# Float32 attention heads by pairs, on the whole TensorE array, in a fused attention and FFN kernel

## The chip, the cores and the metric

The kernel runs on one core of one Trainium2 chip. The metric is device time in microseconds (us) for one execution of the whole program, from loading the inputs to storing the output. The engines of the core are named as in the profile: PE (TensorE matmul), PEld (TensorE's weight loads), DVE (VectorE), ACT (ScalarE), POOL (GpSimd) and SP (SyncE, which here issues nearly all DMA loads and stores).

## The reference, cut to what matters

An attention with a local window and 32 global tokens runs over 8 batches and 8 heads of size 64, with 512 local positions; an FFN with a squared ReLU runs over its 4608 rows.

```python
k_all = concatenate([k_g, k_l]); v_all = concatenate([v_g, v_l])
out_g = softmax(scale * q_g @ k_all.T) @ v_all            # 32 global rows see everything
s_ll  = where(abs(pos_i - pos_j) <= 32, scale * q_l @ k_l.T, -1e9)
s_lg  = scale * q_l @ k_g.T
out_l = softmax(concatenate([s_lg, s_ll])) @ v_all        # local rows see a window and the globals
x = concatenate([out_g, out_l]) -> (4608, 512)            # heads side by side
h = x @ w_in                                              # 512 -> 2048
out = (s * relu(h) ** 2 + b) @ w_out                      # 2048 -> 512
```

All inputs and the output are float32.

## The kernel before, in words

**Steps and slots.** The attention is cut into 128 slots: slot `j` is batch `j // 16`, half `(j // 8) % 2` of the 512 local positions, and head `j % 8`. Each slot has 256 query rows in two blocks of 128, a window of keys of 416 columns in all (two blocks of 192 or 224, with the 32 global keys among them), and four pieces of values of 128 rows. The FFN is cut into 136 steps `m`, eight for each of 17 tiles of 256 rows: `ffn_in` (12 products for each of two groups of 128 hidden features) and `ffn_out`, and step `m` is written `LAG` = 12 slots after slot `m`. One loop over `j` writes all of this out; a scheduler then orders the instructions of each engine with a simulated time line and places the semaphores, so the order on an engine isn't quite the order of the loop.

**Two kinds of heads.** Most products split each float32 operand into a rounded part and a remainder and multiply these in the fast float32r format (`split`, `scores`, `p_split`, `pv_products`, `pv_sum`). The first `NF` = 16 slots (batch 0) don't: they multiply in plain float32, which needs no splitting on ACT, POOL and DVE, while each product is two passes on TensorE, counted as two instructions in the profile. These are the float32 heads, and the change touches only them. They run while the weights of the FFN are being prepared: `weight_piece` takes 32 pieces, two or three a slot over the first 14 slots (`PIECES`), from 64-bit floats to two float32r parts, with four operations on DVE (lines 143, 148, 152, 156), four on ACT or POOL and one more on POOL or DVE. Two pieces are loaded by ACT's queue, the others by SP's.

**One float32 head.** `load32` (line 252) loads the keys of a pair of heads into one tile of 128 partitions (the even head in partitions 0 to 63, the odd one in 64 to 127), and for each head its queries; the array `qd` holds the same queries in both halves of the partitions. `v_load32` (line 268) loads a head's values, 128 x 256. `scores32` (line 274) makes two products of the head's own 64 partitions of queries and keys (line 283) into the scores `ps_s`, and one product (line 289) of its 32 global queries and its own keys into `ps_g`; ACT copies the latter into the global scores `sg` (line 291). Ahead of it, while `j` < 12, four products of a constant tile keep TensorE busy (`keep_busy`, line 91). `softmax` (line 206) masks and scales on DVE (line 215), exponentiates on ACT (line 221), sums on DVE and normalises on POOL (line 228). `transposes32` turns the probabilities by four transposes (line 312), and ACT copies them to `pt` (line 320). `pv32` (line 323) multiplies values by probabilities in four products (line 329) of 64 output partitions, `p_o[0:64]`, and copies these to the head's 64 partitions of `x` (DVE for slots 0 to 7, line 337; ACT for 8 to 15, line 335).

**Buffers.** Score, global-score, transpose and output banks (tags `s`, `g`, `t`, `o`) have one buffer each; probabilities, their transposes and the values (`sm`, `pt`, `rv`) have two. The keys alternate between two tags, the queries as well. SP's queue issues in order, so a load that waits for its buffer holds those behind it.

**Around it.** `x_split` (before FFN tile 0, at slot 12) needs the outputs of slots 0 to 7; the global softmax and products of batch 0 follow slots 13 and 18. The functions that the diff touches:

Of the kernel before, what the change touches and what calls it, by code (L numbers as in the profile page):

```python
# [10 lines left out]
F32 = mybir.dt.float32  # L11
# [31 lines left out]
NF = 16  # L43
# [9 lines left out]
X_ACT = lambda j: j >= 8  # L53
# [11 lines left out]


@with_exitstack
def window_attention_then_ffn(ctx: ExitStack, tc: tile.TileContext, qd, qg, kw, vw, vg, w_in, w_out, sv, bv, out):
    nc = tc.nc
    scale = 1.0 / math.sqrt(D)  # L70

# [1 line left out]
    sb = ctx.enter_context(tc.tile_pool(name="sb", bufs=2))  # L73
    ps = ctx.enter_context(tc.tile_pool(name="ps", bufs=1, space=bass.MemoryType.PSUM))
# [22 lines left out]
    for first, parts in ((True, ((32, 192, 0),)), (False, ((0, 160, 0), (192, 224, 32)))):  # L97
# [108 lines left out]
    def softmax(j, p_s):  # L206
        b, hf, h = slot(j)
        sm = sb.tile([P, NC], F32, tag="sm", name=f"sm{j}")
        nm = sb.tile([P, 2], F32, tag="nm", name=f"nm{j}")
        ss = sb.tile([P, 2], F32, tag="ss", name=f"ss{j}")  # L210
        cols = [COLS[hf, blk] for blk in range(2)]
        for blk in range(2):
            c = cols[blk]
            mask = masks[hf == 0 and blk == 0][:, 0:c.stop - c.start]
            nc.vector.tensor_tensor_reduce(  # L215
                out=sm[:, c], in0=p_s[:, c], in1=mask,
                op0=ALU.add, op1=ALU.min, scale=-scale, scalar=BIG, accum_out=nm[:, blk:blk + 1],
            )
        for blk in range(2):
            p = sm[:, cols[blk]]  # L220
            nc.scalar.activation(  # L221
                out=p, in_=p, func=AF.Exp, bias=nm[:, blk:blk + 1], scale=-1.0, accum_out=ss[:, blk:blk + 1],
            )
        nc.vector.tensor_scalar_add(ss, ss, 1e-9)
        nc.vector.reciprocal(ss, ss)
        for blk in range(2):
            p = sm[:, cols[blk]]
            (nc.gpsimd if NORM_POOL(j) else nc.vector).tensor_scalar(  # L228
                out=p, in0=p, scalar1=ss[:, blk:blk + 1], scalar2=1.0, op0=ALU.mult, op1=ALU.mult,
            )  # L230
        st_["p", j] = sm


    def own(k, hf):
        n, c = (192, P) if hf == 0 else (240, 144)
        return k[:, 0:2 * n].rearrange("p (k c) -> p k c", k=2)[:, :, 0:c]

    def sg_rows(j):
        b, hf, h = slot(j)
        if hf == 0 and h % 4 == 0:  # L240
            st_["sg", b, h // 4] = sb.tile([P, SGW], F32, tag=f"sg{h // 4}", name=f"sg{j}", bufs=1)
        r0 = 32 * (h % 4)
        return st_["sg", b, h // 4][r0:r0 + 32]

    def x_tile(j):
        b, hf, h = slot(j)
        t = 2 * b + hf
        if h == 0:
            xcur[t] = sb.tile([P, 4, HALF], F32, tag="x", name=f"x{t}", bufs=1)
        return xcur[t]  # L250

    def load32(j):
        b, hf, h = slot(j)
        if h % 2 == 0:
            if j % 4 == 0:
                rk = sb.tile([P, 480], F32, tag="rk", name=f"rk{j}", bufs=1)
            else:
                rk = sb.tile([P, 10 * D], F32, tag="rvg", name=f"rk{j}", bufs=1)[:, 0:480]
            nc.sync.dma_start(rk[:, 0:NC], kw[b, hf, h // 2])
            st_["rk", j] = st_["rk", j + 1] = rk  # L260
        if j % 2 == 0:
            rq = sb.tile([P, HALF], F32, tag="rq", name=f"rq{j}", bufs=1)
        else:
            rq = sb.tile([P, 288], F32, tag="tg", name=f"rq{j}", bufs=1)[:, 0:HALF]
        nc.sync.dma_start(rq, qd[b, hf, h])
        st_["rq", j] = rq

    def v_load32(j):
        b, hf, h = slot(j)
        rv = sb.tile([P, 4 * D], F32, tag="rv", name=f"rv{j}")  # L270
        nc.sync.dma_start(rv, vw[b, hf, h])
        st_["rv", j] = rv

    def scores32(j):
        b, hf, h = slot(j)
        if WARM_HEAD and j < LAG:
            keep_busy(WARM_HEAD, f"warm{j + 1}")
        p = slice(64 * (h % 2), 64 * (h % 2) + 64)
        rk, rq = st_.pop(("rk", j)), st_.pop(("rq", j))
        p_s = ps.tile([P, 512], F32, tag="s", name=f"ps_s{j}")  # L280
        for blk in range(2):
            cols = COLS[hf, blk]
            nc.tensor.matmul(  # L283
                p_s[:, cols], lhsT=rq[p, blk * P:(blk + 1) * P], rhs=rk[p, cols], start=True, stop=True,
            )
        p_g = ps.tile([P, 512], F32, tag="g", name=f"ps_g{j}")
        qg = st_["rqg", b][p, h * SG:(h + 1) * SG]
        ng = 256 + 32 * hf
        nc.tensor.matmul(p_g[0:32, 0:ng], lhsT=qg, rhs=own(rk, hf)[p], start=True, stop=True)
        softmax(j, p_s)  # L290
        nc.scalar.copy(out=sg_rows(j)[:, hf * 256:hf * 256 + ng], in_=p_g[0:32, 0:ng])

    def chunks(j):
        b, hf, h = slot(j)
        o = 0
        for blk in range(2):
            for c in range(2):
                c0, q0, n = CHUNKS[hf, blk][c]
                yield blk, c, c0, q0, n, slice(o, o + n)
                o += n  # L300
# [22 lines left out]
    def pv32(j):  # L323
        b, hf, h = slot(j)
        pt, rv = st_.pop(("pt", j)), st_.pop(("rv", j))
        p_o = ps.tile([P, 2, 2, P], F32, tag="o", name=f"ps_o{j}")
        for blk, c, c0, q0, n, o in sorted(chunks(j), key=lambda x: (x[0], -x[1])):
            v = (2 * blk + c) * D
            nc.tensor.matmul(  # L329
                p_o[0:64, 0, blk, q0:q0 + n], lhsT=rv[:, v:v + D], rhs=pt[:, o], start=(c == 1), stop=(c == 0),  # L330
            )
        q0 = 64 * (h % 2)
        x_out = x_tile(j)[q0:q0 + 64, h // 2, :].rearrange("p (k q) -> p k q", k=2)
        if X_ACT(j):
            nc.scalar.copy(out=x_out, in_=p_o[0:64, 0])
        else:
            nc.vector.tensor_copy(out=x_out, in_=p_o[0:64, 0])
# [12 lines left out]
    def qg_split(b):  # L350
# [216 lines left out]
    for b in range(B):  # L567
        for g in range(2):
# [4 lines left out]
            for i in range(2):  # L573
                h = 4 * g + 2 * i
# [3 lines left out]
    def pick(f32_one, split_one):  # L578
# [18 lines left out]
    ld(1)
    for j in range(NM + LAG + 2):
# [6 lines left out]
        if j < NS:  # L605
            b1 = j // 16 + 1
            if j == 14 and NF > 16:
                qg_load32(1)
            elif j % 16 == 14 and b1 < B:
                qg_load(b1)  # L610
            sc(j)
            if j == NF - 1 and NF % 16:
                if NF > 16:
                    qg_load(j // 16)
                qg_split(j // 16)
            if j % 16 == 15 and NF <= j + 1 < NS:
                qg_split(b1)
# [93 lines left out]
```

## Time and profile before

| | |
|---|---|
| median of 3 runs | 1093.29 us (1093.09 to 1093.58) |
| profiled execution | 1092.8 us, span 1091.0 us |
| PE busy | 1052.7 us (96%) |
| PEld busy | 929.0 us (85%) |
| DVE busy | 858.8 us (79%) |
| ACT busy | 724.3 us (66%) |
| POOL busy | 418.3 us (38%) |
| mean granted TensorE clock | 0.974 |
| moved by DMA | 86.80 MB |

The span runs from the first to the last instruction. The granted clock is the share of full speed that TensorE was allowed; a busy TensorE at half clock does half the work. Rows for a group of instructions name the line, the engine, the operation, output and inputs with their shapes, how often, busy us and mean ns, and then the idle time of the engine just before them with what ended it. For a product, `64*128` says that 64 rows and 128 columns of the array are used.

### The profile page before, as it was taken

To read this page: it belongs to the slowest core of one execution; us is meant where nothing else is said; L and a number is where in the kernel's file an instruction comes from. 1 tells how busy PE (TensorE), PEld (TensorE's weight loads), DVE (VectorE), ACT (ScalarE), POOL (GpSimd) and SP (SyncE) were. 2 spreads that over 40 slices of the span, in tenths; PEclk is the share of its full clock that TensorE was granted. 3 is DMA by queue.
4 is the path that set the end of the run, shared out by engine and by line. 5 is a ranking of instruction groups with operands and counts; after the bars stand their busy time and mean duration, and the time that the engine had idled before them with its cause. 6 is when DMAs were issued, how large, how long until landed. Compare 5 with 4: busy or idle time off the path is not lost.

```text
span 1091.0 us, 20690 instructions
## 1 busy us (share of the span) xinstructions
PE 1052.7 (96%) x7121; PEld 929.0 (85%) x7124; DVE 858.8 (79%) x2120; ACT 724.3 (66%) x1828; POOL 418.3 (38%) x457
## 2 busy tenths in 40 slices
PE   8889969999999999999999999999999999999996
PEld 3357758999999999999999999999999999998895
DVE  7979999799778987887888887888788878854221
ACT  5567658687667876786768676786678667744221
POOL 5878765343324433442433342342344334301000
PEclk9759989999999999999999999999999999999999
DMA  6455423132122312231313122221122122200000
GB/s 233 125 156 155 138 80 111 51 109 73 58 69 71 100 57 87 67 99 47 99 55 105 51 87 62 84 82 61 56 90 87 51 83 65 73 13 34 21 20 20
DMA packets 63536, 86.80 MB, mean 80 GB/s; under 512 B 7624, under 2 KB 50632, under 8 KB 63432
## 3 DMA queue, kind: packets, MB, share of 16 engines
q1 hardware_dynamic: 63144, 84.44, 25.3%
q8 instruction: 56, 0.92, 0.4%
q10 hardware_dynamic: 288, 1.05, 0.3%
q14 instruction: 48, 0.39, 0.1%
HBM read 76.02 MB, written 9.44 MB: 78 GB/s over the span
## 4 chain that ended last, share of the span: by engine, by line
PE 83%; DVE 12%; issue 2%; DMA 1%; ACT 1%; POOL 0%; SPq 0%; DVEq 0%; POOLq 0%; ACTq 0%
PE acc L545 32%; PE ps_h L513 32%; PE ps_t L312 5%; PE ps_s L364 4%; PE ps_o L391 4%; DVE wst L152 2%; PE ps_og L465 2%; DVE we L148 2%; DVE wst L156 2%; DVE we L143 2%; PE ps_g L370 1%; DVE sm L215 1%; PE ps_tg L443 1%; PE ps_o L329 1%; PE ps_s L283 1%
## 5 line engine op out<-in xcount | busy, mean ns | idle before, releaser
L513 PE MATMUL ps_h<-xs,wi 128*128 128x256 f32 x3264 | 445.5, 284 | 5.6 <-ACT wi L159 2.0
L545 PE MATMUL acc<-wo,g 128*128 128x512 f32 x1632 | 431.2, 401 | 6.1 <-DVE g L528 4.6
L513 PEld LDWEIGHTS ps_h<-xs,wi 128*128 128x128 f32 x3264 | 416.6, 190 | 18.9 <-ACT wi L159 3.1
L545 PEld LDWEIGHTS acc<-wo,g 128*128 128x128 f32 x1632 | 291.7, 189 | 63.5 <-DVE g L528 6.1
L203 POOL TENSOR_TENSOR vs<-rv,vs 128x256 fp32r<-128x256 f32 x112 | 86.8, 775 | 193.2 <-ACT vs L202 193.0
L520 DVE SCALAR_TENSOR_TENSOR r<-ps_h,s_t,r 128x512 f32<-128x512 f32 x136 | 101.5, 746 | 71.0 <-ACT r L519 70.6
L527 ACT ACTIVATE g<-r,b_t 128x512 fp32r<-128x512 f32 x136 | 98.4, 723 | 70.2 <-DVE r L520 69.8
L528 DVE SCALAR_TENSOR_TENSOR g<-r,b_t,g 128x512 fp32r<-128x512 f32 x136 | 108.6, 799 | 45.5 <-ACT g L527 42.5
L519 ACT ACTIVATE r<-ps_h 128x512 f32<-128x512 f32 x136 | 81.1, 597 | 84.7 <-PE ps_h L513 79.0
L195 POOL TENSOR_TENSOR kq<-rq,kq 128x256 fp32r<-128x256 f32 x112 | 88.8, 793 | 123.8 <-ACT kq L194 111.7
L221 ACT ACTIVATE sm<-sm,nm 128x224 f32<-128x224 f32 (+1 forms) x256 | 118.4, 465 | 21.7 <-DVE nm L215 20.9
L193 POOL TENSOR_TENSOR kq<-rk,kq 64x416 fp32r<-64x416 f32 x56 | 63.1, 1128 | 126.9 <-ACT kq L192 113.1
L312 PE MATMUL ps_t<-ident,sm 128*128 128x128 f32 x512 | 101.0, 287 | 5.9 <-POOL sm L228 5.9
L215 DVE CUSTOM_DVE_ANT_0 sm<-ps_s,mask 128x224 f32<-128x224 f32 (+1 forms) x256 | 85.5, 366 | 17.1 <-PE ps_t L312 11.4
L457 POOL TENSOR_TENSOR vsg<-rvg,vsg 128x320 fp32r<-128x320 f32 x64 | 57.6, 921 | 94.8 <-ACT vsg L456 94.7
L391 PE MATMUL ps_o<-pt,vs 128*128 128x256 f32 x448 | 84.1, 283 | 0.0
L364 PE MATMUL ps_s<-kq 128*128 128x192 f32 (+1 forms) x448 | 74.1, 276 | 0.8 <-DVE nm L215 0.7
L228 DVE TENSOR_SCALAR sm<-sm,ss 128x192 f32<-128x192 f32 (+1 forms) x224 | 70.4, 356 | 3.3
L405 DVE TENSOR_TENSOR x<-u 64x256 f32<-64x256 f32 x112 | 69.6, 621 | 3.6
L364 PEld LDWEIGHTS ps_s<-kq 128*128 128x128 f32 x448 | 65.8, 190 | 6.9 <-ACT vsg L456 1.0
L312 PEld LDWEIGHTS ps_t<-ident,sm 128*128 128x128 f32 x512 | 58.1, 144 | 14.8 <-POOL sm L228 8.5
L391 PEld LDWEIGHTS ps_o<-pt,vs 128*128 128x128 f32 x448 | 67.4, 190 | 2.2
(85 smaller groups left out, 1394.3 us busy)
## 6 DMA issues: line engine op xcount, KB each, us to landing
rq<-in_qd SPq DMA_DIRECT2D x128, 128.0 KB, 2.2
rv<-in_vw SPq DMA_DIRECT2D x128, 128.0 KB, 2.1
rk<-in_kw SPq DMA_DIRECT2D x64, 208.0 KB, 2.4
rvg<-in_vg SPq DMA_DIRECT2D x32, 320.0 KB, 3.0
out<-o SPq DMA_DIRECT2D x34, 256.0 KB, 2.2
wst<-in_w_in SPq DMA_DIRECT2D x15, 512.0 KB, 3.7
wst<-in_w_out SPq DMA_DIRECT2D x15, 512.0 KB, 4.4
rqg<-in_qg SPq DMA_DIRECT2D x8, 128.0 KB, 2.1
```

Source lines behind the costliest of these rows:

```text
L195: nc.gpsimd.tensor_sub(out=qs[:, 1, :], in0=rq, in1=f32(qs[:, 0, :]))
L203: nc.gpsimd.tensor_sub(out=vs[:, :, 1, :], in0=rv4, in1=f32(vs[:, :, 0, :]))
L215: nc.vector.tensor_tensor_reduce(out=sm[:, c], in0=p_s[:, c], in1=mask, op0=ALU.add, op1=ALU.min, scale=-scale, scalar=BIG, accum_out=nm[: ...
L221: nc.scalar.activation(out=p, in_=p, func=AF.Exp, bias=nm[:, blk:blk + 1], scale=-1.0, accum_out=ss[:, blk:blk + 1],)
L312: nc.tensor.transpose(out=p_t[:, at:at + P], in_=sm[:, c0:c0 + P], identity=ident)
L364: nc.tensor.matmul(p_s[:, cols], lhsT=qs[:, a, blk * P:(blk + 1) * P], rhs=ks[:, cols], start=(a == 0), stop=(a == 1),)
L391: nc.tensor.matmul(p_o[:, blk, :, q0:q0 + n], lhsT=vs[:, 2 * blk + c], rhs=pt[:, :, o], start=(c == 1), stop=(c == 0),)
L513: nc.tensor.matmul(p_h[:, k], lhsT=wi[:, a, c, f * P:(f + 1) * P], rhs=xs[:, e, c, :], start=(n == 0), stop=(n == 11),)
L520: nc.vector.scalar_tensor_tensor(out=r, in0=p_h, scalar=s_t, in1=r, op0=ALU.mult, op1=ALU.mult)
L527: nc.scalar.activation(out=g[:, 0], in_=r, func=AF.Identity, bias=b_t)
L528: nc.vector.scalar_tensor_tensor(out=g[:, 1], in0=r, scalar=b_t, in1=f32(g[:, 0]), op0=ALU.add, op1=ALU.subtract,)
L545: nc.tensor.matmul(oacc[t][i], lhsT=g[:, a, k, i * P:(i + 1) * P], rhs=wo[:, e, f, :], start=(pr == 0 and n == 0), stop=(pr == 7 and n == 5),)
```

## The change

For the float32 heads three new input arrays are made on the host. `qz` holds the queries of a head only in its own 64 partitions, with zeros in the other head's; `qgz` does the same with the global queries; `vz` holds the values with 128 columns for each piece, the head's 64 in its own half and zeros in the other.

- The scores' products read all 128 partitions of queries and keys; the zeros cancel the other head's keys.
- The global scores of a pair are one product at the odd head, with the 64 global queries of both heads, into 64 partitions, copied at once.
- The value products write all 128 partitions. Both heads of a pair add into one bank (the first product clears it, the other head's half gets zeros added), and one copy of 128 x 256 at the odd head brings both to `x`.
- A head's values are 128 x 512 rather than 128 x 256, in tiles of their own (`rvz`, two buffers).

```diff
@@ load32, v_load32 @@
-        nc.sync.dma_start(rq, qd[b, hf, h])
+        nc.sync.dma_start(rq, qz[j])
...
-        rv = sb.tile([P, 4 * D], F32, tag="rv", name=f"rv{j}")
-        nc.sync.dma_start(rv, vw[b, hf, h])
+        rv = sb.tile([P, 8 * D], F32, tag="rvz", name=f"rv{j}")
+        nc.sync.dma_start(rv, vz[j])
@@ scores32 @@
-        p = slice(64 * (h % 2), 64 * (h % 2) + 64)
...
-                p_s[:, cols], lhsT=rq[p, blk * P:(blk + 1) * P], rhs=rk[p, cols], start=True, stop=True,
+                p_s[:, cols], lhsT=rq[:, blk * P:(blk + 1) * P], rhs=rk[:, cols], start=True, stop=True,
...
-        p_g = ps.tile([P, 512], F32, tag="g", name=f"ps_g{j}")
-        qg = st_["rqg", b][p, h * SG:(h + 1) * SG]
-        ng = 256 + 32 * hf
-        nc.tensor.matmul(p_g[0:32, 0:ng], lhsT=qg, rhs=own(rk, hf)[p], start=True, stop=True)
+        rows = sg_rows(j)
+        if h % 2 == 1:
+            p_g = ps.tile([P, 512], F32, tag="g", name=f"ps_g{j}")
+            ng = 256 + 32 * hf
+            two = st_["rqg", b][:, (h - 1) * SG:(h + 1) * SG]
+            nc.tensor.matmul(p_g[0:64, 0:ng], lhsT=two, rhs=own(rk, hf), start=True, stop=True)
         softmax(j, p_s)
-        nc.scalar.copy(out=sg_rows(j)[:, hf * 256:hf * 256 + ng], in_=p_g[0:32, 0:ng])
+        if h % 2 == 1:
+            r0 = 32 * (h % 4 - 1)
+            rows = st_["sg", b, h // 4][r0:r0 + 64]
+            nc.scalar.copy(out=rows[:, hf * 256:hf * 256 + ng], in_=p_g[0:64, 0:ng])
@@ pv32 @@
-        p_o = ps.tile([P, 2, 2, P], F32, tag="o", name=f"ps_o{j}")
+        odd = h % 2 == 1
+        if not odd:
+            st_["pso", j + 1] = ps.tile([P, 2, P], F32, tag="o", name=f"ps_o{j}")
+        p_o = st_["pso", j] if odd else st_["pso", j + 1]
...
-            v = (2 * blk + c) * D
+            v = (2 * blk + c) * P
             nc.tensor.matmul(
-                p_o[0:64, 0, blk, q0:q0 + n], lhsT=rv[:, v:v + D], rhs=pt[:, o], start=(c == 1), stop=(c == 0),
+                p_o[:, blk, q0:q0 + n], lhsT=rv[:, v:v + P], rhs=pt[:, o],
+                start=(not odd and blk == 0 and c == 1), stop=(odd and blk == 1 and c == 0),
             )
...
+        if odd:
+            p_o = st_.pop(("pso", j))
+            x_out = x[:, h // 2, :].rearrange("p (k q) -> p k q", k=2)
             if X_ACT(j):
-                nc.scalar.copy(out=x_out, in_=p_o[0:64, 0])
+                nc.scalar.copy(out=x_out, in_=p_o)
             else:
-                nc.vector.tensor_copy(out=x_out, in_=p_o[0:64, 0])
+                nc.vector.tensor_copy(out=x_out, in_=p_o)
```

The load of the first batch's global queries reads `qgz` in place of `qg`.

More of the change, by code (lines that the diff above doesn't have):

```diff
@@ L67, in window_attention_then_ffn @@
 @with_exitstack
-def window_attention_then_ffn(ctx: ExitStack, tc: tile.TileContext, qd, qg, kw, vw, vg, w_in, w_out, sv, bv, out):
+def window_attention_then_ffn(ctx: ExitStack, tc: tile.TileContext, qd, qg, kw, vw, vg, qz, qgz, vz, w_in, w_out, sv, bv, out):
     nc = tc.nc
@@ L264, in load32 @@
             rq = sb.tile([P, 288], F32, tag="tg", name=f"rq{j}", bufs=1)[:, 0:HALF]
-        nc.sync.dma_start(rq, qd[b, hf, h])
+        nc.sync.dma_start(rq, qz[j])
         st_["rq", j] = rq
     def v_load32(j):
-        b, hf, h = slot(j)
-        rv = sb.tile([P, 4 * D], F32, tag="rv", name=f"rv{j}")
-        nc.sync.dma_start(rv, vw[b, hf, h])
+        rv = sb.tile([P, 8 * D], F32, tag="rvz", name=f"rv{j}")
+        nc.sync.dma_start(rv, vz[j])
         st_["rv", j] = rv
@@ L325, in pv32 @@
         pt, rv = st_.pop(("pt", j)), st_.pop(("rv", j))
-        p_o = ps.tile([P, 2, 2, P], F32, tag="o", name=f"ps_o{j}")
+        odd = h % 2 == 1
+        if not odd:
+            st_["pso", j + 1] = ps.tile([P, 2, P], F32, tag="o", name=f"ps_o{j}")
+        p_o = st_["pso", j] if odd else st_["pso", j + 1]
         for blk, c, c0, q0, n, o in sorted(chunks(j), key=lambda x: (x[0], -x[1])):
-            v = (2 * blk + c) * D
+            v = (2 * blk + c) * P
             nc.tensor.matmul(
-                p_o[0:64, 0, blk, q0:q0 + n], lhsT=rv[:, v:v + D], rhs=pt[:, o], start=(c == 1), stop=(c == 0),
-            )
-        q0 = 64 * (h % 2)
-        x_out = x_tile(j)[q0:q0 + 64, h // 2, :].rearrange("p (k q) -> p k q", k=2)
-        if X_ACT(j):
-            nc.scalar.copy(out=x_out, in_=p_o[0:64, 0])
-        else:
-            nc.vector.tensor_copy(out=x_out, in_=p_o[0:64, 0])
+                p_o[:, blk, q0:q0 + n], lhsT=rv[:, v:v + P], rhs=pt[:, o],
+                start=(not odd and blk == 0 and c == 1), stop=(odd and blk == 1 and c == 0),
+            )
+        x = x_tile(j)
+        if odd:
+            p_o = st_.pop(("pso", j))
+            x_out = x[:, h // 2, :].rearrange("p (k q) -> p k q", k=2)
+            if X_ACT(j):
+                nc.scalar.copy(out=x_out, in_=p_o)
+            else:
+                nc.vector.tensor_copy(out=x_out, in_=p_o)
     def qg_load(b):
         rqg = sb.tile([P, H * SG], F32, tag="xr", name=f"rqg{b}", bufs=1)
-        nc.sync.dma_start(rqg, qg[b])
+        nc.sync.dma_start(rqg, qgz[0] if b == 0 else qg[b])
         st_["rqg", b] = rqg
@@ L346, in qg_load32 @@
         rqg = sb.tile([P, n], F32, tag="rqg", name=f"rqw{b}", bufs=1)
-        nc.sync.dma_start(rqg, qg[b, :, 0:n])
+        nc.sync.dma_start(rqg, qgz[b, :, 0:n])
         st_["rqg", b] = rqg
@@ L688 @@
     vg = _np.ascontiguousarray(vg).reshape(B, H // 2, P, 10 * D)
+    qz, qgz = qd.reshape(-1, 2, P, HALF)[0:NF // 2].copy(), qg[0:2].reshape(2, P, H // 2, 2, SG).copy()
+    vz = _np.zeros((NF // 2, 2, P, 4, 2, D), dt)
+    for i in range(2):
+        other = slice(64 - 64 * i, 128 - 64 * i)
+        qz[:, i, other] = 0
+        qgz[:, other, :, i] = 0
+        vz[:, i, :, :, i] = vw.reshape(-1, 2, P, 4, D)[0:NF // 2, i]
+    qz, qgz, vz = qz.reshape(NF, P, HALF), qgz.reshape(2, P, H * SG), vz.reshape(NF, P, 8 * D)
     w_in = a["moe_w_in"].reshape(DM // P, P, DF // P, P).transpose(2, 1, 0, 3)
@@ L695 @@
     ins = {
-        "qd": qd, "qg": qg, "kw": kw, "vw": vw, "vg": vg, "w_in": w_in, "w_out": w_out,
+        "qd": qd, "qg": qg, "kw": kw, "vw": vw, "vg": vg, "qz": qz, "qgz": qgz, "vz": vz, "w_in": w_in, "w_out": w_out,
         "sv": a["moe_s"], "bv": a["moe_b"],
@@ L704 @@
     args.append(nc.dram_tensor("out_0", (B * (SL + SG), DM), F32, kind="ExternalOutput").ap())
-    for i in (5, 6):
+    for i in (8, 9):
         args[i] = args[i].bitcast(I32)
```

## The prediction

> **What bounds the kernel now.** I read the stretches of the span first (columns: busy time and count on PE, PEld, DVE, ACT and POOL, then granted TensorE clock, DMA share, GB/s).
>
> ```profile
> span 1091.0 us, 20690 instructions
> ...
> 0.00:48.00 48.00, 39.20 (x149) 17.24 (x152) 40.30 (x74) 28.45 (x62) 32.26 (x36) 0.93 0.58 188
> 48.00:84.00 36.00, 30.91 (x108) 19.13 (x109) 28.63 (x69) 22.65 (x54) 27.15 (x26) 0.57 0.50 155
> 84.00:176.00 92.00, 78.30 (x438) 61.84 (x437) 91.61 (x152) 62.31 (x138) 70.07 (x56) 0.93 0.38 117
> 176.00:1050.00 874.00, 872.72 (x6241) 803.14 (x6240) 690.71 (x1818) 603.08 (x1564) 288.87 (x341) 1.00 0.23 70
> ```
>
> From 176 us on TensorE is full at full clock, and nothing of the change lies there: the float32 heads are the first 16. What counts is how early that state is reached. From 84 to 176 us VectorE is full (91.61 of 92) with the weight pieces, so TensorE, 13.7 us idle there, sets nothing. Between 48 and 84 us neither is full: VectorE idles 36 − 28.63 = 7.4 us, and TensorE, busy 30.91 of 36, has a mean clock of 0.57. So I take this stretch by operation and form (count, busy us, mean ns; then idle time ahead and who ended it):
>
> ```profile
> L215 DVE CUSTOM_DVE_ANT_0 sm<-ps_s,mask 128x224 f32<-128x224 f32 x6 | 2.3, 389 | 2.7 <-PE ps_t L312 2.7
> L215 DVE CUSTOM_DVE_ANT_0 sm<-ps_s,mask 128x192 f32<-128x192 f32 x6 | 2.1, 353 | 3.0 <-PE ps_t L312 1.3 <-POOL sm L228 1.1 <-PE ps_s L283 0.6
> L337 DVE COPY x<-ps_o 64x256 f32<-64x256 f32 x5 | 2.1, 416 | 1.1 <-PE ps_o L329 1.0
> L283 PE MATMUL ps_s<-rk,rq 64*128 64x224 f32 x12 | 5.4, 545 | 1.8 <-DVE nm L215 1.8
> L289 PE MATMUL ps_g<-rk,rqg 64*32 64x288 f32 x10 | 5.3, 628 | 1.5 <-DMA rk<-in_kw 1.5
> L329 PE MATMUL ps_o<-pt,rv 128*64 128x128 f32 x20 | 6.1, 407 | 0.6 <-ACT pt L320 0.6
> L283 PEld LDWEIGHTS ps_s<-rk,rq 64*128 64x128 f32 x23 | 5.8, 280 | 3.6 <-DVE nm L215 2.6 <-DVE we L143 0.3 <-DVE ss L224 0.2
> L329 PEld LDWEIGHTS ps_o<-pt,rv 128*64 128x64 f32 x40 | 6.0, 202 | 4.4 <-issue 2.1 <-ACT pt L320 1.9 <-ACT sm L221 0.4
> ```
>
> VectorE's idle time is largely waiting for TensorE: 2.7 + 1.3 + 0.6 + 1.0 = 5.6 us, behind transposes, scores and value products of the float32 heads. The slow TensorE is therefore on the path exactly here.
>
> Why is its clock at half? I cut the stretch at the times where the clock changes, which lie multiples of 3.4 us apart:
>
> ```profile
> 51.90:55.30 3.40, 3.40 (x12) 1.60 (x10) 3.36 (x4) 1.17 (x4) 3.04 (x2) 0.50 0.00 0
> 55.30:58.70 3.40, 3.40 (x11) 1.92 (x11) 2.78 (x9) 2.10 (x5) 2.10 (x2) 0.50 0.25 74
> ...
> 65.50:68.90 3.40, 2.22 (x14) 1.55 (x14) 2.55 (x10) 3.29 (x9) 1.76 (x3) 1.00 0.25 96
> 68.90:72.30 3.40, 2.80 (x10) 1.35 (x9) 2.63 (x9) 1.51 (x5) 2.66 (x4) 0.50 0.81 229
> 72.30:75.70 3.40, 3.40 (x14) 2.35 (x12) 2.29 (x5) 2.94 (x9) 2.57 (x2) 0.50 0.52 196
> ...
> 79.10:82.50 3.40, 3.40 (x14) 2.17 (x14) 3.34 (x5) 1.28 (x4) 2.84 (x2) 0.50 0.59 176
> 82.50:85.90 3.40, 2.52 (x16) 1.56 (x14) 3.06 (x10) 3.38 (x10) 1.51 (x3) 0.99 0.38 139
> ```
>
> TensorE is busy all through four of these windows (those from 51.9, 55.3, 72.3 and 79.1), all at half clock, and only after the last of them does the clock rise. What ran in them, by the order of time on TensorE (start, duration):
>
> ```profile
> 52.15 0.48 PE L312 MATMUL ps_t<-ident,sm 128*128 128x128 f32 x1
> 52.56 0.48 PE L329 MATMUL ps_o<-pt,rv 128*64 128x64 f32 x2
> ...
> 55.32 1.75 PE L283 MATMUL ps_s<-rk,rq 64*128 64x192 f32 x4
> 57.00 1.17 PE L289 MATMUL ps_g<-rk,rqg 64*32 64x288 f32 x2
> 58.09 1.65 PE L329 MATMUL ps_o<-pt,rv 128*64 128x128 f32 x8
> ...
> 79.03 1.65 PE L329 MATMUL ps_o<-pt,rv 128*64 128x128 f32 x8
> 80.61 1.17 PE L289 MATMUL ps_g<-rk,rqg 64*32 64x288 f32 x2
> 81.70 1.06 PE L312 MATMUL ps_t<-ident,sm 128*128 128x128 f32 x4
> ```
>
> Weigh busy time by array rows used. From 55.3: scores 1.7 us and global scores 1.1 us on 64 of 128 rows, value products 0.6 us on all rows: 0.85 + 0.55 + 0.6 = 2.0 us, 59% of the window; half clock stays. From 79.1: value products 1.5, global 0.55, transposes 0.8: 2.85 us, 84%; the clock rises. From 51.9, transposes and value products alternate, 0.41 us a transpose where four in a row take 1.06 (0.26 each): counted without that loss, about 70%; it stays. So filling the rows looks like what the clock asks for, somewhere between 70 and 84%. I choose this reading; weighing by columns fails, since the scores fill all 128 and the window from 55.3 would then lead the one from 79.1.
>
> [...]
>
> **The change part by part.** *Scores.* Same instructions and columns, 128 rows in place of 64. No duration should grow: value products on 128 rows stream 416 columns twice in 1.58 us (79.03 to 80.61), scores on 64 rows the same columns in 1.68 (55.32 to 57.00). Cost 0; but what the scores weigh for the clock doubles (5.4 us busy in this stretch for the wide ones alone).
>
> *Global scores.* One product a pair, the same 256 or 288 columns: half of 5.3 us goes here, 2.65 us of TensorE. Half of the ScalarE copies behind them go too; ScalarE, 22.65 of 36 busy, is not the bound, so 0.
>
> *Value products.* As many, writing 128 columns of the array, so each loads 128 columns of weights in place of 64: 202 ns becomes 280 by the scores' loads. For 40 loads +3.1 us at half clock if each lies bare, 0 if hidden behind the previous matmul (407 ns for the long ones). I take half, +1.6; against −2.65 that leaves TensorE work at about −1, part of the waits below. [...]
>
> *Outputs.* The even head's copy disappears; the odd one covers 128 partitions. The nearest whole-height PSUM row says that it is not dearer:
>
> ```profile
> L403 DVE TENSOR_TENSOR u<-ps_o,u 128x256 f32<-128x256 f32 x112 | 46.6, 416 | 4.4 <-ACT u L402 3.9
> ```
>
> 416 ns, like the copy above. Four of the eight copies on VectorE go (heads 0 to 7), **−1.7 us** on the engine that sets the pace; four on ScalarE cost nothing. The output bank is held over two heads, but the next pair's first product waits for one copy as now. Price 0.
>
> *Loads.* Queries and first global queries keep their size; the 16 value loads double.
>
> ```profile
> rv<-in_vw SPq DMA_DIRECT2D x128, 128.0 KB, 2.1
> ...
> 8.00:12.00 4.00, 3.96 (x19) 1.74 (x16) 3.81 (x6) 1.39 (x3) 1.61 (x1) 1.00 1.07 352
> ...
> 7.84 0.71 SPq L271 DMA_DIRECT2D rv<-in_vw  x1
> 8.80 0.33 SPq L137 DMA_DIRECT2D wst<-in_w_out  x1
> ...
> SPq L271 <- PE ps_o L329: 27.6, 9, 8.2
> SPq L265 <- PE ps_s L283: 17.7, 9, 3.4
> ```
>
> From 8 to 12 us the DMA engines are full at 352 GB/s, and the first value load is issued ahead of weight pieces. Two value loads' extra 262 KB are 0.7 us there; VectorE follows the pieces closely. I take **+0.4**. All 2.1 MB at 352 GB/s would be 6.0 us, were every load in a weight piece's way; after 16 us the DMA share is about one half, so I go by the low end. The load queue's own waits for value products and scores (the last two rows) shorten with a faster TensorE, and the weight pieces queued behind them come no later.
>
> *The waits.* If the clock comes back, TensorE's chain from 48 to 84 us (30.91 busy at 0.57) shortens by well over the 5.6 us that VectorE waits for it. But some comes back as the next wait: 1.1 us above belongs to POOL, and TensorE itself waits 1.5 us for a pair's keys to land (the idle time of line 289 above), which no clock shortens. I take two thirds of 5.6: **−3.7 us**, between 0 and 6.7 (POOL's 1.1 too). What becomes late next is VectorE itself, full as after 84 us.
>
> **Sum**: −1.7 + 0.4 − 3.7 = −5.0. The profiled execution took 1092.8 us (span 1091.0 and 1.8 around it), so 1087.8; the runs' median 1093.29 lies 0.5 above, so **1088.3 us**. Its own range: −1.7 − 6.7 = −8.4 to −1.7 + 0.7 = −1.0, that is 1084.9 to 1092.3. The instruction order comes from a scheduler with its own time estimates, which sees other instructions here; TensorE's 9.4 us of idle time after 1050 us
>
> ```profile
> 1050.00:1091.00 41.00, 31.59 (x191) 27.61 (x190) 7.51 (x10) 7.79 (x12) 0.00 (x0) 0.94 0.04 13
> ```
>
> shows where an order can cost or give a microsecond or two. I let the range reach 1.9 us further below.
>
> **The rivals.** *The clock stays at half* (0.20). For it: float32 work alone may never satisfy the clock, and alternating windows stay near 70% whatever the rows. Against it: the rise at 82.5 came from float32 work alone. Then only −1.7 + 0.4 and a part of TensorE's −1 remain: about 1091.5.
>
> *The wait moves on* (0.15): the clock rises, but loads and POOL keep VectorE waiting, as 27.15 of POOL's 36 us busy and the load-queue waits suggest; against it, POOL's idle 8.8 us still leave room. A quarter of the 5.6 us is recovered: −1.7 + 0.4 − 1.4, about 1090.6.
>
> *Slower* (0.15): the larger value loads delay weight pieces. Place: the load queue up to 130 us; price up to 6.0 us of transfers, less the 1.7: 1093.3 + 4.3 = 1097.6. It decides once VectorE's first weight operation (line 143) waits over 2 us in all for pieces after the first one. For it, the DMA share of 1.07; against it, the 0.50 in the stretch that matters.
>
> **How the numbers follow.** The forecast has 0.50. What a measurement of this kernel can tell from no change is about 0.2%, 2.2 us. Faster by more: 0.46 of the forecast's 0.50, 0.07 of the first rival, 0.10 of the second: 0.63. Slower by more: 0.11 of the third and 0.03 of the first two's bad order: 0.14. The rest, 0.23, is within. The range 1083.0 to 1095.5 holds the forecast, two rivals and the milder half of the slower one.
>
> **What would show it.** The clock's mean from 48 to 84 us well above 0.57; VectorE's waits for TensorE there under 2 us; eight copies to the outputs, four on VectorE; 16 global matmul instructions with all rows; value loads' landing time. A clock near 0.57 with a gain, or a full clock with VectorE's idle time unchanged, would prove the main step wrong; so would a VectorE that gets longer between 84 and 176 us.

## The result and the profile after

The changed kernel takes **1086.38 us** (median of 8 runs, 1085.06 to 1088.17) against 1093.39 us before (8 runs beside them, 1089.28 to 1093.75): a ratio of 0.994, with a 95% interval of 0.9928 to 0.9953, so 7.0 us less. Its profiled execution took 1085.6 us, that of before 1092.8. Eight runs of before range over 4.5 us, so a difference of 2 us between two single profiles settles nothing by itself.

The stretches of the span after the change; the last row starts where VectorE's last weight operation (line 156) ends:

```profile
span 1083.7 us, 20628 instructions
...
0.00:48.00 48.00, 35.14 (x157) 19.65 (x158) 40.23 (x77) 28.52 (x63) 35.43 (x41) 0.95 0.63 212
48.00:84.00 36.00, 24.22 (x112) 18.59 (x112) 35.90 (x70) 23.91 (x56) 28.60 (x26) 0.74 0.61 184
84.00:157.30 73.30, 60.83 (x357) 53.19 (x356) 72.94 (x121) 48.69 (x105) 56.69 (x45) 0.88 0.45 133
157.30:1083.70 926.40, 913.73 (x6487) 838.42 (x6485) 710.44 (x1852) 619.33 (x1596) 297.55 (x348) 1.00 0.23 67
```

The kernel before, cut at its own last weight operation (the first two stretches stand in the prediction):

```profile
84.00:164.20 80.20, 67.67 (x379) 53.93 (x378) 80.03 (x124) 53.02 (x113) 61.88 (x49) 0.91 0.39 121
164.20:1091.00 926.80, 914.94 (x6489) 838.66 (x6487) 709.80 (x1856) 620.16 (x1601) 297.05 (x348) 1.00 0.22 67
```

The pair of last rows says where the time went. What follows the last weight operation is the same to 0.4 us (926.8 and 926.4); that operation ends 6.9 us earlier, at 157.3 in place of 164.2. Up to it VectorE is busy for 40.30 + 28.63 + 80.03 = 149.0 us before and 40.23 + 35.90 + 72.94 = 149.1 after, so its work has not shrunk: its idle time has, from 15.2 to 8.2 us, and all of that between 48 and 84 us (7.37 before, 0.10 after).

The same stretch, 48 to 84 us, by operation and form:

```profile
L215 DVE CUSTOM_DVE_ANT_0 sm<-ps_s,mask 128x224 f32<-128x224 f32 x5 | 1.9, 375 | 0.0
L215 DVE CUSTOM_DVE_ANT_0 sm<-ps_s,mask 128x192 f32<-128x192 f32 x5 | 1.7, 345 | 0.0
L346 DVE COPY x<-ps_o 128x256 f32<-128x256 f32 x3 | 1.2, 411 | 0.0
L281 PE MATMUL ps_s<-rk,rq 128*128 128x224 f32 x10 | 3.9, 484 | 2.1 <-DVE nm L215 2.1
L289 PE MATMUL ps_g<-rk,rqg 128*64 128x288 f32 x6 | 3.1, 620 | 0.0
L335 PE MATMUL ps_o<-pt,rv 128*128 128x128 f32 x16 | 4.2, 351 | 5.0 <-ACT pt L323 5.0
L335 PEld LDWEIGHTS ps_o<-pt,rv 128*128 128x128 f32 x32 | 4.8, 225 | 5.8 <-ACT pt L323 5.8
```

VectorE's 5.6 us of waits for TensorE are gone (0.0 in the first three rows). The direction has turned: TensorE waits for VectorE's masking (2.1) and ScalarE's copies (5.0). The clock's mean is 0.74 in place of 0.57, but half clock did not vanish. Two windows of it, cut as in the prediction:

```profile
73.90:77.30 3.40, 3.40 (x12) 2.44 (x10) 3.40 (x5) 1.60 (x3) 1.81 (x2) 0.50 0.27 80
77.30:80.70 3.40, 0.74 (x6) 0.59 (x6) 3.40 (x11) 1.99 (x4) 2.51 (x3) 1.00 0.76 208
```

After one full window (busy for all of its 3.40 us, at 0.50) the clock stands at 1.00, as the prediction reads it; by then TensorE has so little to do (0.74 us in the next window) that the full clock carries little work. So the result alone leaves open whether the clock or the smaller work took the waits away. The experiments go after that.

### The profile page after: what moved, and what is told of

Its sections match the earlier page's. It is cut to its first block, busy times and chain, and to the rows that moved or that the text cites. A ratio compares the mean times of both kernels' runs of the same rounds, so it can differ in the third digit from the quotient of the medians.

```text
span 1083.7 us, 20628 instructions
## 1 busy us (share of the span) xinstructions
PE 1033.9 (95%) x7108; PEld 929.8 (86%) x7108; DVE 859.5 (79%) x2116; ACT 720.4 (66%) x1816; POOL 418.3 (39%) x457
## 4 chain that ended last, share of the span: by engine, by line
PE 82%; DVE 13%; issue 2%; DMA 1%; ACT 1%; POOL 0%; POOLq 0%; DVEq 0%; ACTq 0%
PE ps_h L522 33%; PE acc L554 33%; PE ps_t L315 5%; PE ps_s L373 4%; PE ps_o L400 4%; DVE we L148 3%; DVE we L143 2%; DVE wst L152 2%; PE ps_og L474 2%; DVE wst L156 2%; PE ps_g L379 1%; DVE sm L215 1%; PE ps_tg L452 1%; DVE ss L224 1%; DVE g L537 1%
## 5 line engine op out<-in xcount | busy, mean ns | idle before, releaser
L315 PE MATMUL ps_t<-ident,sm 128*128 128x128 f32 x512 | 96.7, 279 | 5.8 <-POOL sm L228 5.8
L228 DVE TENSOR_SCALAR sm<-sm,ss 128x192 f32<-128x192 f32 (+1 forms) x224 | 72.6, 366 | 3.2
```

The costliest lines, as they stand in the source:

```text
L315: nc.tensor.transpose(out=p_t[:, at:at + P], in_=sm[:, c0:c0 + P], identity=ident)
```

## The experiments

**1. What raises the clock: forms of product by themselves.** Behind the unchanged kernel a tail holds ScalarE copies that leave TensorE idle, and then one burst of a single form: 18 float32 products of 256 columns (36 instructions), or 64 transposes; each form once from a resting TensorE and once right behind 30 bfloat16 products.

```diff
+    for form in ((64, 128), (128, 128), (128, 64), (64, 32), (128, 32), "T"):   # rows, columns
+        for warmed in range(2):
+            quiet(p_w)                       # 15 copies on ACT
...
+            if warmed:
+                for _ in range(30):
+                    nc.tensor.matmul(p_w, lhsT=warm[:, 0:P], rhs=Rb, start=True, stop=True)
...
+        for _ in range(18):
+            nc.tensor.matmul(p_w[0:cols, 0:256], lhsT=ident[0:rows, 0:cols], rhs=R[0:rows, 0:256], start=True, stop=True)
```

> The kernel before with a tail behind its last output (the outputs stay the reference's; the total time is longer by the tail and is not compared). In the tail TensorE is left idle for over 8 us while ScalarE copies, then runs 18 float32 products of 256 columns of one form without a gap; then the same again with 30 bfloat16 products ahead of them, so that the form starts at full clock. Forms (rows x columns of the array): 64x128, 128x128, 128x64, 64x32, 128x32, and 64 whole-array transposes. Rows decide (my theory): 64x128 and 64x32 stay at 0.50 from a cold start to the end of the burst; 128x128, 128x64 and 128x32 rise to 1.00 within 3.4 to 7 us. Columns decide (rival): 64x128 rises, 128x64 and 128x32 do not. Busy time alone decides (rival): all rise. Float32 never counts (rival): none rises. Durations should be the same for 64 and 128 rows in every theory.

Stretches of the bursts: 64 rows from rest, 64 rows from full clock, 128 x 128 from rest (two parts), 64 x 32 from rest, 128 x 32 from rest (two parts):

```profile
1101.50:1117.00 15.50, 15.50 (x36) 11.78 (x36) 0.00 (x0) 0.52 (x1) 0.00 (x0) 0.50 0.00 1
1135.80:1143.70 7.90, 7.90 (x37) 6.60 (x36) 0.00 (x0) 0.00 (x0) 0.00 (x0) 1.00 0.00 0
1153.20:1159.50 6.30, 6.30 (x17) 5.12 (x18) 0.00 (x0) 0.57 (x1) 0.00 (x0) 0.58 0.00 0
1159.50:1163.80 4.30, 4.30 (x21) 3.48 (x19) 0.00 (x0) 0.00 (x0) 0.00 (x0) 1.00 0.00 0
1248.10:1263.50 15.40, 15.40 (x36) 6.07 (x36) 0.00 (x0) 0.57 (x1) 0.00 (x0) 0.50 0.00 0
1299.80:1305.50 5.70, 5.70 (x14) 2.31 (x15) 0.00 (x0) 0.52 (x1) 0.00 (x0) 0.52 0.01 3
1305.50:1310.40 4.90, 4.90 (x23) 2.31 (x21) 0.00 (x0) 0.00 (x0) 0.00 (x0) 1.00 0.00 0
```

On 64 rows TensorE is busy for 15.5 us without a gap (15.4 with 32 columns) and the clock stays at 0.50: busy time alone did not raise it. On 128 rows it is full after 5.4 to 6.1 us, with 128 columns and with 32 alike. In these bursts rows decide the rise, columns do not; this is the reading that the prediction chose. But 64 rows from full clock keep 1.00 for the whole 7.9 us: they did not raise it in 15.5 us, and they did not lower it in 7.9. (The stationary operand of these bursts is an identity matrix; whether other data would act the same was not tried.)

**2. The parts alone.** Three kernels from the one before, each with one part of the change: only the scores on 128 rows, only the joint global product, only the pair's value products with their single copy.

```diff
@@ scores alone @@
-                p_s[:, cols], lhsT=rq[p, blk * P:(blk + 1) * P], rhs=rk[p, cols], start=True, stop=True,
+                p_s[:, cols], lhsT=rq[:, blk * P:(blk + 1) * P], rhs=rk[:, cols], start=True, stop=True,
@@ global product alone @@
+        if h % 2 == 1:
...
+            two = st_["rqg", b][:, (h - 1) * SG:(h + 1) * SG]
+            nc.tensor.matmul(p_g[0:64, 0:ng], lhsT=two, rhs=own(rk, hf), start=True, stop=True)
@@ value products alone @@
+                p_o[:, blk, q0:q0 + n], lhsT=rv[:, v:v + P], rhs=pt[:, o],
+                start=(not odd and blk == 0 and c == 1), stop=(odd and blk == 1 and c == 0),
```

> The kernel before with only the scores' products on whole rows (queries with zeros); global products, value products, copies and value loads as before. No work is removed. Clock theory: the mean clock between 48 and 84 us rises from 0.57 to over 0.70, VectorE's waits for TensorE there fall from 5.6 us to under 3, and the time falls by 2.5 to 5 us, to 1088.3 to 1090.8. Work theory (the gain is the four VectorE copies and the eight global products removed): no change, 1092.3 to 1094.3.

> The kernel before with only the global scores by pairs (one product of all rows at the odd head, one copy), the rest as before. Work theory: TensorE loses eight products of about 1.1 us at half clock, and the time falls by 2 us or more, to under 1091.3. Clock theory: what counts are full rows in busy windows; a pair's product counts as much as its two half-row products did, so the clock stays near 0.57 and the time falls by at most 1.5 us, 1091.8 to 1093.4.

> The kernel before with only the value products by pairs (128 columns, one bank and one copy a pair, value loads of 256 KB). Clock theory by rows: rows stay as they were, so only the copies' 1.7 us less the loads' 0.4 come: 1091.5 to 1092.5. Work theory: the copies are most of the gain: 1089 to 1091. Third theory (changes of shape between transposes and value products cost TensorE time): the alternating windows fill up, the clock between 48 and 84 us goes over 0.65 and the time falls by over 3 us.

Measured: scores alone 1089.94 us, ratio 0.9972 (0.996 to 0.9985); global product alone 1091.28, 0.9989 (0.9978 to 1.0001); value products alone 1093.46, 1.0005 (0.9993 to 1.0017). That is −3.2, −1.8 and 0.3 us, together −4.7, where the whole gave −7.0; the intervals of the last two include a ratio of 1. Scores alone land in the range of the clock theory, but without its clock (over 0.70) and without its fall of the waits; the value products alone land above all three expectations. The stretch from 48 to 84 us of scores alone:

```profile
48.00:84.00 36.00, 29.43 (x112) 18.66 (x112) 28.71 (x71) 22.68 (x57) 27.91 (x25) 0.64 0.49 149
```

Its VectorE groups in that stretch:

```profile
L215 DVE CUSTOM_DVE_ANT_0 sm<-ps_s,mask 128x224 f32<-128x224 f32 x6 | 2.3, 386 | 3.4 <-PE ps_t L312 3.4
L215 DVE CUSTOM_DVE_ANT_0 sm<-ps_s,mask 128x192 f32<-128x192 f32 x6 | 2.1, 350 | 1.4 <-POOL sm L228 1.1 <-PE ps_s L283 0.3
L337 DVE COPY x<-ps_o 64x256 f32<-64x256 f32 x5 | 2.1, 417 | 2.3 <-PE ps_o L329 2.3
```

And on its TensorE's time line the start of a new pair of heads:

```profile
65.67 0.64 PE L289 MATMUL ps_g<-rk,rqg 64*32 64x288 f32 x2 [3.51 <-DMA rk<-in_kw]
```

Here every engine has the very order of before, and only the rows of the scores differ. The clock rises (0.64 for 0.57), but VectorE's waits stay: 3.4 + 0.3 + 2.3 = 6.0 us. TensorE gets to the next pair sooner, and there stands 3.51 us for its keys, where before stood 1.54 us. (This profile is of the slowest of its twelve executions, 1091.7 us; the median gained more than the profile shows.)

The same stretch of the global product alone:

```profile
48.00:84.00 36.00, 26.11 (x98) 16.96 (x98) 35.37 (x74) 22.85 (x53) 27.32 (x27) 0.63 0.53 164
```

That of the value products alone, and then the group of their copies:

```profile
48.00:84.00 36.00, 32.58 (x109) 21.88 (x109) 30.35 (x68) 23.37 (x58) 24.06 (x24) 0.56 0.50 161
```

```profile
L342 DVE COPY x<-ps_o 128x256 f32<-128x256 f32 x3 | 1.2, 415 | 3.1 <-PE ps_o L331 3.1
```

With the global product alone VectorE is busy for 35.37 of 36 us at nearly the same clock as with the scores alone: with half of these products (and an order of its own) the waits are gone. Its last weight operation still ends at 162.4 us: VectorE is idle for 9.4 us up to there, so busy for 153.0, 4 us more than before, and most of the gain is given back in longer operations. The value products alone keep 5.6 us of waits (3.1 of them in the row above), and TensorE is busier than before, 32.58 for 30.91, as are its weight loads, 21.88 for 19.13. For these two kernels the scheduler wrote other orders of instructions, so neither shows its edit by itself.

**3. The change without one part.** Scores back on 64 rows, all else as changed; and the pair's outputs copied in two halves of 64 partitions, as many copies as before.

```diff
@@ scores on 64 rows @@
-                p_s[:, cols], lhsT=rq[:, blk * P:(blk + 1) * P], rhs=rk[:, cols], start=True, stop=True,
+                p_s[:, cols], lhsT=rq[p, blk * P:(blk + 1) * P], rhs=rk[p, cols], start=True, stop=True,
@@ two copies @@
+            for k in range(2):
+                r = slice(64 * k, 64 * k + 64)
+                x_out = x[r, h // 2, :].rearrange("p (k q) -> p k q", k=2)
...
```

> The changed kernel with the scores' products back on a head's own 64 rows; global pairs, value pairs, single copies and large value loads stay. Clock theory: the clock between 48 and 84 us falls back to under 0.65, VectorE waits for TensorE again by over 2.5 us, and the time rises by 2.5 to 5 us over the changed kernel, to 1089 to 1091.5. Work theory: nothing that costs time is put back: 1085.5 to 1087.5.

> The changed kernel with each pair's output copied by two instructions of 64 partitions in place of one of 128. Work theory, and my sum's term for the copies: VectorE, full from 8 us on, does four copies of 0.41 us more: plus 1.2 to 2.0 us, 1087.6 to 1088.4. If VectorE's order has room after all: no change, within 0.7 us of 1086.4.

Measured: 1087.06 us, ratio 0.9949 (0.9934 to 0.9964), and 1088.25, 0.996 (0.9945 to 0.9975). Without the full rows of the scores nearly the whole gain stays, as the work theory had it, although the clock is back at 0.59. The two copies cost 1.9 us over the changed kernel, near the 1.7 us put down for them, though the intervals of the two ratios overlap. In both the scheduler had written another order of instructions, hundreds of them moved, so an edit and an order were mixed; the last experiment takes them apart.

**4. The larger value loads alone.** The kernel before, loading 128 x 512 for each head into tiles of their own and using the same 64 columns of each piece.

```diff
+        rv = sb.tile([P, 8 * D], F32, tag="rvz", name=f"rv{j}")
+        nc.sync.dma_start(rv, vz[j])
...
+            v = (2 * blk + c) * P + D * (h % 2)
```

> The kernel before with only the value loads doubled (256 KB a head, into tiles of their own; half of what is loaded is not used). Isolates the load term: my sum has plus 0.4 us, 1093.3 to 1094.0. The slower rival (weight pieces come late) has up to plus 6 us: over 1095.5.

Measured: 1088.72 us, ratio 0.9959 (0.9946 to 0.9972). An edit that only adds 2.1 MB of loads made the kernel 4.5 us faster, where both expectations had it slower or the same. (It has no usable profile: the profiled execution took 3316.9 us and is left out of the median of the other eight.) It seemed that this could not be the loads' own doing, so the order of instructions became a suspect of its own.

**5. A high clock without less work.** The kernel before with twice the constant products that keep TensorE busy, over 16 slots.

```diff
+WARM_TO = 16
...
-WARM_HEAD = 4
+WARM_HEAD = 8
...
-        if WARM_HEAD and j < LAG:
+        if WARM_HEAD and j < WARM_TO:
```

> The kernel before with eight bfloat16 products of a constant tile ahead of each of the 16 float32 heads, in place of four ahead of the first twelve: 80 more products, about 17 us of TensorE at full clock, and nothing else. Clock theory: the mean clock between 48 and 84 us goes over 0.80, VectorE's waits for TensorE there fall under 3 us, and the time falls by 1 to 4 us although TensorE has more to do: 1089.3 to 1092.3. Work theory: more work on the engine that VectorE waits for: over 1094.

Measured: 1095.33 us, ratio 1.0028 (1.0016 to 1.004). Its stretches:

```profile
48.00:84.00 36.00, 31.84 (x142) 18.10 (x143) 34.67 (x68) 23.59 (x54) 30.16 (x24) 0.81 0.54 157
...
155.70:1093.30 937.60, 925.36 (x6541) 845.99 (x6539) 714.82 (x1860) 624.25 (x1608) 300.46 (x351) 1.00 0.23 67
```

The clock is the highest of all kernels (0.81), VectorE hardly waits, and the last weight operation ends at 155.7 us, earlier than after the change. But 937.6 us are left then, 10.8 more than before: TensorE did filler when it could have done FFN products, and those come later (6541 TensorE instructions are left then, 6489 before). The clock and the waits came as the clock theory had them, the time as the work theory had it: here a clock bought with filler costs more than it brings.

**The kernel before against itself.** The profile of experiment 1 holds a second execution of the kernel before: up to the tail, every engine has the same instructions in the same order. In this one the clock stayed at half through the whole stretch:

```profile
48.00:84.00 36.00, 31.93 (x105) 19.70 (x106) 26.03 (x64) 20.47 (x51) 26.59 (x25) 0.50 0.44 138
```

VectorE idles 9.97 us there in place of 7.37, and its last weight operation ends at 166.3 us in place of 164.2; ScalarE's last copy into an output tile ends 2.1 us later too (1084.3 for 1082.2). So for the work of before, with nothing else changed, a lower clock goes with a later end. The 29 executions of before that were timed beside experiment 2 lean the same way: the seven fastest (1089.3 to 1090.5 us) have mean clocks of 0.973 to 0.980, the others (1092.2 to 1095.0 us) 0.966 to 0.977.

**6. One order for all.** In four kernels each instruction is tied to the one that stood before it on its engine in another kernel; the tie orders and adds no wait. Where an instruction of the pattern doesn't exist, its place is left out.

```diff
+        for _names in _order.values():          # one list for each engine
+            for _a, _b in zip(_names, _names[1:]):
+                tc.add_manual_dep(nc.get_inst_by_name(f"I-{_b}"), f"I-{_a}", _info, reason="order")
```

The work of before (values in tiles of their own, their old size) in the order of experiment 4; experiment 4's loads in the order of before; the whole change in the order of before; and scores on 64 rows in the order of the changed kernel:

> The kernel before, its values loaded at their old size into tiles of their own, with every engine's instructions held in exactly the order that the scheduler gave the kernel with doubled value loads (which took 1088.72 us). Nothing is computed or loaded differently from the kernel before. Order theory (the 4.5 us of that kernel came from the order that the scheduler chose when it saw longer loads): 1087.5 to 1090. Load theory (something in the larger loads or their tiles helps): 1092.5 to 1094.

> The doubled value loads with every engine held in the order of the kernel before. Order theory: no gain is left, and what remains is the price of the loads themselves, my sum's plus 0.4 us: 1093.0 to 1094.2. Load theory: 1087.5 to 1090. The slower rival (weight pieces come late): over 1095.5.

> The changed kernel with every engine held in the order of the kernel before, the removed instructions left out. Content theory (full rows, half the global products, fewer copies bring the 7 us by themselves): 1085.5 to 1087.5. Mixed theory (rows alone brought 3.2 us in this very order; copies 1.7 by my sum and 1.9 measured; the rest is a better order): 1087.8 to 1090. Order theory (nearly all is order): over 1091.

> The changed kernel with the scores back on 64 rows and every engine held in the changed kernel's own order; only the rows of 32 products differ from it. If full rows are worth what they were in the order before (3.2 us): 1088.6 to 1090.6. If the new order hides a slow clock, or the value products and pairs fill the windows without the scores: within 1 us of 1086.4.

| work | order | us | ratio (95%) | VectorE's last weight operation ends |
|---|---|---|---|---|
| before, own value tiles | of exp. 4 | 1088.35 | 0.9954 (0.9938 to 0.997) | 157.7 |
| before, double value loads | of before | 1089.31 | 0.9965 (0.9952 to 0.9977) | 160.6 |
| whole change | of before | 1087.37 | 0.9948 (0.9934 to 0.9962) | 158.9 |
| change, scores on 64 rows | of after | 1087.14 | 0.9948 (0.9934 to 0.9963) | 159.2 |

The whole change in before's order, its stretches:

```profile
48.00:84.00 36.00, 27.03 (x120) 21.09 (x120) 34.34 (x73) 24.81 (x60) 31.68 (x28) 0.69 0.56 177
...
158.90:1085.90 927.00, 915.29 (x6491) 839.20 (x6489) 707.85 (x1857) 619.79 (x1602) 297.00 (x348) 1.00 0.23 67
```

The change with scores on 64 rows, its stretches, and then the one VectorE group from 48 to 84 us with a wait for TensorE:

```profile
48.00:84.00 36.00, 27.47 (x103) 19.98 (x103) 34.23 (x69) 23.07 (x55) 26.76 (x25) 0.59 0.58 182
...
159.20:1085.50 926.30, 913.83 (x6487) 838.39 (x6485) 710.43 (x1852) 618.66 (x1596) 297.74 (x348) 1.00 0.23 67
```

```profile
L215 DVE CUSTOM_DVE_ANT_0 sm<-ps_s,mask 128x192 f32<-128x192 f32 x5 | 1.8, 351 | 1.7 <-PE ps_t L316 1.7
```

Three things follow. The change itself, not the order that it happened to get, makes 6.4 of the 7 us (third line). The double loads into tiles of their own are a part of it, and they alone give 4.5 us in this very order (second line); all the rest adds 1.9 us to that, with intervals that overlap. The full clock is not what the changed work needs (fourth line): at 0.59, TensorE is still done early enough for VectorE to be busy 34.23 of 36 us, and the time is 0.8 us from the changed kernel's, within the intervals. And the same work in another order, with value tiles of its own, gains 5.5 us (first line) without any other part of the change; the order and the tiles were not tried apart.

The second line surprised most: with the same instructions in the same order, doubling the value loads (in tiles of their own) gains 4.5 us. Its 1089.31 us lie where the fastest executions of before lie. What the traces show of it: before, TensorE stands until 66.68 us for the keys of the next pair (1.54 us, quoted in the prediction in line 289's row). With the double loads the keys are there and the product starts without a wait, still at half clock; then the clock rises, as it did before, but it stays full through the window from 68.9 us, which before was at half (a row of the prediction). The place on TensorE's time line, and that window:

```profile
64.21 1.17 PE L288 MATMUL ps_g<-rk,rqg 64*32 64x288 f32 x2
```

```profile
68.90:72.30 3.40, 2.64 (x16) 1.82 (x16) 3.37 (x11) 2.85 (x9) 3.40 (x4) 1.00 0.88 342
```

The keys were issued at 60.98 us, 0.85 us earlier, and landed in 3.1 us in place of 4.7. The issues from 55 to 70 us have them in one row each (number, size, us to landing), with the double loads:

```profile
rk<-in_kw SPq DMA_DIRECT2D x1, 208.0 KB, 3.1
```

and before:

```profile
rk<-in_kw SPq DMA_DIRECT2D x1, 208.0 KB, 4.7
```

VectorE is busy for 32.47 us of the stretch from 48 to 84, in place of 28.63. Why, by the tiles of their own or by their size, no run separates: the old size in own tiles and in before's order was not tried.

**Why keys are late.** While a value load waits for TensorE's value products, the load queue issues nothing: before, from 46.8 to 55.0 us, the 8.2 us of a row of the prediction. The keys stand behind such loads in it. A slow TensorE therefore makes its own next keys late. The issue of the keys for the same pair, before:

```profile
61.83 0.43 SPq L259 DMA_DIRECT2D rk<-in_kw  x1
```

and with the whole change in before's order:

```profile
57.13 0.42 SPq L259 DMA_DIRECT2D rk<-in_kw  x1
```

It is 4.7 us earlier: the value loads wait less for TensorE (23.2 us in all up to 140 us, 30.7 before), and no wait for keys is left on TensorE's time line between 58 and 76 us. This reading comes from the traces; no run moved the keys' load alone.

## Why the prediction was right or wrong

**The place and what sets the end: right.** The gain is that VectorE's last weight operation ends 6.9 us earlier, with the rest unchanged (926.8 and 926.4), and the idle time that went is that of 48 to 84 us.

**The forecast of 1088.3 us** is 1.9 us above the 1086.38 measured, which lies inside its own range of 1084.9 to 1092.3. That it is so close is in part luck: the waits were put 3.6 us too low, and against that the 1.7 us of the copies did not come out as less work for VectorE.

**The waits: right in what goes, too low in how much, and wrong in what it needs.** Put at −3.7, two thirds of 5.6 us, "if the clock comes back". All 5.6 went, and POOL's 1.1 too: VectorE's idle time fell from 7.37 to 0.10 us, past the bound of 6.7. The clock did rise, to 0.74. But by the prediction's own test, "a clock near 0.57 with a gain", the main step, that the waits go because the clock comes back, fails: scores on 64 rows give 0.59 and 1087.14 us. The bursts bear out the reading of the clock itself, that rows in use decide (0.50 through 15.5 us on 64 rows, 1.00 after 5.4 to 6.1 us on 128); so do two windows of before that the prediction left out, the one from 58.7 us (busy 3.40 us, half of that on 64 rows; the next window stays at 0.50) and the one from 62.1 (busy 3.04 us, all on 128 rows; the next is at 1.00). A clock raised without less work kept the waits in its profile (scores alone, 0.64 and 6.0 us) or was paid for later (the filler, 0.81 and 1095.33 us). Scores alone did gain 3.2 us in the median, and the kernel before ended 2.1 us later with its clock at half, so the clock counts for a TensorE that has all its old work; beside the other parts full rows add some 0.8 us, within the intervals.

**The mis-sized term** is, as far as the traces tell, the work taken off TensorE, "about −1, part of the waits". Groups of global products up to 170 us, before and after:

```profile
L289 PE MATMUL ps_g<-rk,rqg 64*32 64x288 f32 x16 | 7.3, 548 | 1.5 <-DMA rk<-in_kw 1.5
...
L289 PE MATMUL ps_g<-rk,rqg 64*32 64x256 f32 x16 | 4.9, 386 | 1.7 <-ACT sg L291 1.5
```

```profile
L289 PE MATMUL ps_g<-rk,rqg 128*64 128x288 f32 x8 | 3.8, 573 | 0.0
L289 PE MATMUL ps_g<-rk,rqg 128*64 128x256 f32 x8 | 2.6, 401 | 0.9 <-ACT sg L294 0.5 <-DMA rk<-in_kw 0.4
```

7.3 + 4.9 = 12.2 us become 6.4, at both clocks, and the waits for keys and copies ahead of them shrink from 3.2 to 0.9 us. The value products' weight loads, put at 280 ns and half exposed, are 225 ns here (at a mean clock of 0.74); with 5.8 us of waits of its own ahead of these very loads, TensorE has room for them. The prediction set the one against the other and kept −1. With the global product alone the waits are gone, but in another order and for a gain of 1.8 us only, so how much of the 7 us this term makes is argued, not shown.

**The copies (−1.7): the price right, the use not.** Four copies on VectorE in place of eight, 411 ns at whole height. But VectorE's busy time up to its last weight operation stayed at 149 us, because weight operations took longer. Their four groups up to 170 us, before:

```profile
L152 DVE TENSOR_SCALAR wst<-wst 128x512 int32<-128x512 int32 x32 | 29.9, 946 | 0.2
L148 DVE SCALAR_TENSOR_TENSOR we<-wst,we 128x512 int32<-128x512 int32 x31 | 28.6, 930 | 1.1 <-ACT we L146 1.1
L143 DVE TENSOR_SCALAR we<-wst 128x512 int32<-128x512 int32 x31 | 26.6, 863 | 5.7 <-DMA wst<-in_w_in 5.4 <-DMA wst<-in_w_out 0.3
L156 DVE SCALAR_TENSOR_TENSOR wst<-wst 128x512 f32<-128x512 f32 x32 | 26.1, 827 | 0.3
```

and after:

```profile
L148 DVE SCALAR_TENSOR_TENSOR we<-wst,we 128x512 int32<-128x512 int32 x31 | 33.9, 1098 | 2.0 <-ACT we L146 2.0
...
L156 DVE SCALAR_TENSOR_TENSOR wst<-wst 128x512 f32<-128x512 f32 x32 | 28.3, 888 | 0.2
L143 DVE TENSOR_SCALAR we<-wst 128x512 int32<-128x512 int32 x31 | 26.7, 871 | 4.8 <-DMA wst<-in_w_in 4.6 <-DMA wst<-in_w_out 0.2
L152 DVE TENSOR_SCALAR wst<-wst 128x512 int32<-128x512 int32 x32 | 25.2, 798 | 0.3
```

The sum of the four is 111.2 us before and 114.1 after: 2.9 us come back here, line 148 up and line 152 down. In both traces the operations of line 148 with no GpSimd operation beside them took at most 0.69 us, and all longer ones, up to 1.79 us, ran beside one, while 27 of the 55 that ran beside one took no more than 0.69 us either; no run isolates that as the cause.

**The loads (+0.4): not seen.** The idle time ahead of line 143's pieces is 5.7 before and 4.8 after, and the double loads alone made no kernel slower (1088.72 and 1089.31 us). With that the slower rival falls: the pieces never waited its 2 us more. The first rival, the clock at half, is wrong as a fact (0.74) and, in scores on 64 rows, nearly true without its result: 1087.14 where it gave 1091.5. The second rival, the wait moves on, did not happen to the whole change, but it is what happened to the scores alone: the clock came, TensorE's wait for keys grew from 1.54 to 3.51 us, and 1089.94 us is close to its 1090.6.

**The stretch after 84 us.** VectorE is full there as before and not longer, 72.94 of 73.3 us; that sign of failure stayed away.

**What stays open:** how the 7 us divide among the parts. The parts alone give −3.2, −1.8 and 0.3, and double loads alone −4.5: they all draw on the same idle time of VectorE, 7.37 us in one stretch, and can't be added. The order that the kernel happened to get, and the tiles of their own for the values, are in most of these numbers too.

## What to carry to other kernels

Judge such a change by two numbers: when the engine that sets the pace is done with its share, and how much is left then; a higher clock or a fuller engine is no gain if the second number grows. Work removed from a chain that another engine waits for may be worth more than its own microseconds: by these traces it counts at the slow clock's price (a wide global product took 1.17 us at half clock and 0.64 at full, before) and brings the next loads forward (with the whole change in before's order, the keys were issued 4.7 us earlier); how much of the 7.0 us that made was not shown. Where a scheduler writes the order, compare edits in one pinned order: the same work in another order, with one set of tiles moved, was worth nearly as much here as the edit (5.5 of 7.0 us).

## What the runs showed of the hardware

- Float32 products on 64 rows did not raise TensorE's clock (0.50 over 15.5 us without a gap); on 128 rows they did in 5.4 to 6.1 us, with 32 columns as with 128; 64 rows held a full clock for at least 7.9 us.
- 64 float32 transposes in a row raised it too, after 6.1 us (mean 0.51 in the first row, 1.00 in the second):

```profile
1347.10:1353.20 6.10, 6.10 (x30) 6.10 (x31) 0.00 (x0) 0.51 (x1) 0.00 (x0) 0.51 0.01 3
1353.20:1357.00 3.80, 3.80 (x37) 3.74 (x35) 0.00 (x0) 0.00 (x0) 0.00 (x0) 1.00 0.00 0
```

- Executions of the kernel before spread widely: 29 of them in one batch lay between 1089.3 and 1095.0 us, 0.5% apart, the seven fastest at a mean clock of 0.973 to 0.980, the others at 0.966 to 0.977. Why the clock differs was not isolated.
